# Activating A21 in place in PSUM, and sharing the four Winograd sums out anew between VectorE and GpSimd

## The chip, the cores and the metric

One core of a Trainium2 chip runs the kernel. The metric is device time in microseconds (us) of one execution. The engines are named as in the profile: PE is TensorE (its weight loads are listed apart, as PEld), DVE is VectorE, ACT is ScalarE, POOL is GpSimd, SP is SyncE, which only issues DMAs here. SBUF is the working memory. PSUM is the memory that PE writes its products to; it has eight banks of 512 fp32 columns over 128 partitions.

## The reference

```python
X = np.fft.fft(np.fft.fft(x, axis=1), axis=2).real     # x is 8 x 3008 x 256
h = X.reshape(24064, 256) @ w_in                        # w_in is 256 x 2048
g = h * (1.0 / (1.0 + np.exp(-1.702 * h)))              # quick gelu
return g @ w_out                                        # w_out is 2048 x 256
```

All of it is in fp32.

## The kernel before, in words

**Tiling.** The Fourier transform over the sequence is made by small matrix products (`mix1` and `stage2`), and the one over the 256 features is folded into `w_in` (tiles `wcs`). The rest, the two large products with the gelu between them, is cut into 384 steps. A step `t` is a batch (8), a block of rows (3), a half of it (2) and a place `p` in a group of 8 (line 508). A group shares one tile of output; its step number `p` handles hidden units 256p to 256p + 255 for 256 columns of rows (226 in one group of six). The first 8 steps use a plain form. This text is about steps 8 to 383, in the form below.

**A step.** The transform is symmetric, so each row comes with a mirrored row: the product with `wcs[0]` plus that with `wcs[1]` is the hidden value of one, their difference that of the other. A step has one PSUM bank, `b0` or `b1` by turns, called `x`. Five things happen to it, in this order:

- `middle(t)` (line 592, ACT): two instructions of 256 columns fill `x` with a correction term. I call this the **fill**.
- `begin(t)` (line 599 and the helper's line 184, PE): 8 matmuls add the product with `wcs[0]`.
- `doubled(t)` (line 604, ACT) copies twice that to a tile `g` in SBUF.
- `begin(t, 1)`: 8 more matmuls add the product with `wcs[1]`. `x` now holds the one half.
- `forward(t)` (line 607, ACT) writes the gelu of `x` to blocks A11 and A12 in SBUF. `backward(t)` (line 565, DVE) writes `g - x`, reversed in runs of 32, to blocks A21 and A22 in SBUF. `activate_back(t)` (line 614, ACT) takes the gelu of A21 and A22 in place, as one instruction of 512 columns.

**The sums.** The product with `w_out` is made by Winograd's form of Strassen's scheme, 2 x 2 blocks with seven products. It needs S1 = A21 + A22, S3 = A11 - A21, S2 = S1 - A11 and S4 = A12 - S2 (`sums`). Before, GpSimd makes S1 and S3 at each step (lines 622 and 623, 256 columns each), and VectorE makes S2 and S4 for two steps at once, one step after the odd one (lines 629 and 630, 512 columns each). One of the seven products is itself done by the same scheme over a pair of steps. Its four sums are made by `deeper` on VectorE (line 651, four instructions of 512 columns in each pair): s3, s1 and s2 two steps after the odd step of the pair, s4 one step later.

**Rings.** A11, A21, S3 and S2 lie in a ring of four steps ("left"), A12, S4, A22 and S1 in one of six ("right"). The products of step `t` are made at step `t + 3` (`LAG`).

**Order.** There is no planner: each engine has one queue, in the order of the calls in the loop at line 989. In a step `t` that order is:

- PE: `begin(t, 1)`; the first two of step t-3's large products; `begin(t+1)`; small products; the third large product. At p = 3 the order is another: small products come ahead of `begin(t+1)`.
- ACT: `forward(t)`; at p = 4 the three copies of `swap` (lines 794 to 796); `doubled(t+1)`; `activate_back(t)`; the fill for `t+2`; at p = 2 two copies (lines 754 and 756).
- DVE: `backward(t)`; at p = 3 the four instructions of `combine_small` (line 786); then at even `t` S2 and S4 of two steps and s4, at odd `t` s3, s1 and s2; at p = 2 lines 757 and 758, at p = 4 lines 768 and 804 (`combine_last`), at p = 5 and 6 a transpose (line 737).
- POOL: S1 and S3; in two groups of most batches also the folds of the next batch's input (`fold1`, lines 218 to 231).

A step at whose end `mix1` or `stage2` runs is *special*: that work uses the bank of step `t`, and the fill for `t+2` is issued at the start of the next step.

The fill for `t+2` writes the bank that step `t` used, so it waits until every reader of `x` of step `t` is done:

```python
x = xb[t] = bank("x", f"b{t % 2}")
```

Of the kernel before, what the change touches and what calls it, by code (L numbers as in the profile page):

```python
# [29 lines left out]
ALU = mybir.AluOpType  # L30
ACTF = mybir.ActivationFunctionType
# [19 lines left out]
def free(ap, offset, *dims):  # L51
    return bass.AP(ap.tensor, ap.offset + offset, [list(ap.ap[0])] + [list(d) for d in dims])
# [60 lines left out]
def kernel(ctx: ExitStack, tc, x, w_in, w_out, tab1, tab2, out):  # L113
    nc = tc.nc
# [12 lines left out]
    op = ctx.enter_context(tc.tile_pool(name="op", bufs=2, space=SB))  # L127
# [25 lines left out]
    big = cv.tile([128, 19 * 1024], F32, tag="big", name="big")  # L153
# [353 lines left out]
    NP = NF // 2  # L507
    steps = [(b, blk, hh, p) for b in range(B) for blk in range(NBLK) for hh in range(2) for p in range(NP)]
    vb, ht, xb, gt, pot = {}, {}, {}, {}, {}
    LEFT, MADE, RIGHT, SUM, RES, OUT = 0, 4096, 8192, 14336, 16384, 18432  # L510
    A11, A21, S3, S2 = range(4)
    A12, S4, A22, S1 = range(4)
# [3 lines left out]
    def width(t):  # L516

        return 226 if steps[t][1:3] == (0, 1) else 256
# [20 lines left out]
    def at_left(t, q):  # L539
        return LEFT + t % 4 * 1024 + q * 256  # L540

    def at_right(t, q):
        return RIGHT + (t // 2 % 3 * 2 + t % 2) * 1024 + q * 256

    def left(t, q, n):
        return big[:, at_left(t, q):at_left(t, q) + n]

    def right(t, q, n):
        return big[:, at_right(t, q):at_right(t, q) + n]
# [5 lines left out]
    def back(t):  # L555
        at = at_left(t, A21)
        return free(big[:], at, [at_right(t, A22) - at, 2], [1, width(t)])

    def reversed_sum(out, by, x, y, n, op):

        full, rest = divmod(n, RUN)
        for at, blocks, m in ((0, full, RUN), (full * RUN, 1, rest)):
            if m:
                ins = [free(z[:], at, [256, 2], [RUN, blocks], [1, m]) for z in (x, y)]
                nc.vector.tensor_tensor(free(out, at + m - 1, [by, 2], [RUN, blocks], [-1, m]), *ins, op=op)  # L565
# [19 lines left out]
    def middle(t):  # L585

        b, blk, hh, p = steps[t]
        n = width(t)
        x = xb[t] = bank("x", f"b{t % 2}")
        for i in range(2):  # L590
            f = 2 * p + i
            nc.scalar.activation(x[:, i * 256:i * 256 + n], nbt[b, blk][:, hh * 256:hh * 256 + n], ACTF.Copy,  # L592
                                 scale=af1[:, f:f + 1])

    def begin(t, cs=0):

        n = width(t)
        for i in range(2):
            halves(xb[t][:, i * 256:i * 256 + n], *operands(t, cs, i), start=False, stop=(cs == 1))
# [8 lines left out]

    def backward(t):
        at = at_left(t, A21)  # L610
        reversed_sum(big[:, at:at + 256], at_right(t, A22) - at, gt.pop(t), xb.pop(t), width(t), ALU.subtract)

    def activate_back(t):
        nc.scalar.activation(back(t), back(t), ACTF.Gelu_apprx_sigmoid)  # L614

    def sums(t, eng):

        if not NP <= t < len(steps):
            return
        n = width(t)  # L620
        if eng is nc.gpsimd:
            eng.tensor_tensor(right(t, S1, n), left(t, A21, n), right(t, A22, n), op=ALU.add)  # L622
            eng.tensor_tensor(left(t, S3, n), left(t, A11, n), left(t, A21, n), op=ALU.subtract)  # L623
            return
        if t % 2 == 0:
            return
        a11, s2 = (free(big[:], at_left(t - 1, q), [1024, 2], [1, n]) for q in (A11, S2))
        a12, s4, s1 = (free(big[:], at_right(t - 1, q), [1024, 2], [1, n]) for q in (A12, S4, S1))
        eng.tensor_tensor(s2, s1, a11, op=ALU.subtract)  # L629
        eng.tensor_tensor(s4, a12, s2, op=ALU.subtract)  # L630

    def deep(t):

        return NP <= t < last

    def raws(t, half):

        return free(big[:], at_right(t, 0) + half * (width(t) // 2), [256, 4], [1, width(t) // 2])

    def made_sum(q, w):  # L640
        return free(big[:], SUM + 512 * q, [128, 4], [1, w])

    def deeper(t, part):

        if t < 0 or not deep(t) or not steps[t][3] % 2:
            return
        s1, s2, s3, s4 = (made_sum(q, width(t) // 2) for q in range(4))
        a11, a12, a21, a22 = (raws(k, half) for half in range(2) for k in (t - 1, t))
        for out, i0, i1, how in (((s3, a11, a21, ALU.subtract), (s1, a21, a22, ALU.add), (s2, s1, a11, ALU.subtract)),
                                 ((s4, a12, s2, ALU.subtract),))[part]:  # L650
            nc.vector.tensor_tensor(out, i0, i1, op=how)  # L651

    SPOT = {2: 0, 6: 1, 5: 2, 7: 3, 3: 4, 4: 5}
# [282 lines left out]
    n = len(steps)  # L936
# [52 lines left out]
    for t in range(n + LAG):  # L989
        if t < NP:  # L990
            if t == NP - 3:
                spare[:] = [tag for tag in spare if tag[0] == "o"] + ["b2"]
            if t == NP - 1:
                middle(NP)
            hidden(t)
            if t == NP - 1:
                begin(NP)
                no_row(1024)
            if t == 0:
                squares(in2, nc.scalar)  # L1000
                nyquist(0, 0)
                low_up(in2)
                low_down(in2)
            if t in rows_at:
                first_row(rows_at[t])
            if t >= LAG and t != LAG + 1:
                product(t - LAG, 0, None)
            if t == LAG:
                product(1, 0, None)
            if t == 5:  # L1010
                bounds(("out", 2))
            if t == 6:
                low_down(("out", 3))
            if t:
                activate(t - 1)
            if t == 3:
                bounds(("in", 3))
            if t == 5:
                bounds(("out", 3), False)
            if t in early:  # L1020
                fold_w(early[t])
            rows(t)
            if t == NP - 1:
                doubled(NP)
                middle(NP + 1)
        else:
            after, special = (any(fn in (mix1, stage2) for fn, _ in extra.get(k, ())) for k in (t - 1, t))
            if t < n:
                begin(t, 1)
            if t == NP:  # L1030
                activate(t - 1)
            if after and t + 1 < n:
                middle(t + 1)
            if t < n:
                forward(t)
            while waiting:
                m, ps = waiting.pop()
                mixed(m, 1, ps)
            opening = (t - LAG) % NP == 0 and t >= NP + LAG
            one, other = (t - LAG, (1, 2, 4, 7)), (t - LAG - 1, (5, 6, 3))  # L1040
            if opening:
                small_products(*other)
            cut = 0 if opening and not after else 3 if after else 2
            product(t - LAG, 0, cut)
            if after:
                small_products(one[0], one[1][:1])
                small_products(other[0], () if opening else other[1][:1])
            if t + 1 < n:
                begin(t + 1)
            if not opening:  # L1050
                small_products(other[0], other[1][after:])
            product(t - LAG, cut, 6 if t - LAG == last else None)
            small_products(one[0], one[1][after:])
            swap(t - LAG - 2)
            if t < n:
                backward(t)
            if t + 1 < n:
                doubled(t + 1)
            if t < n:
                activate_back(t)  # L1060
                sums(t, nc.gpsimd)
            if t + 2 < n and not special:
                middle(t + 2)
            combine_small(t - LAG - 1)
            if t - LAG == last:
                product(last, 6, None)
            sums(t - 1, nc.vector)
            deeper(t - 2, 0)
            deeper(t - 3, 1)
        if t == NP:  # L1070
            psu.close()
            low = ctx.enter_context(tc.tile_pool(name="low", bufs=1, space=PS))
            pot["low"] = low.tile([128, 3 * 512], F32, tag="low", name="low")
        if t >= LAG:
            combine(t - LAG)
            combine_last(t - LAG - 2)
            turn_last(t - LAG - 3, 0)
            turn_last(t - LAG - 4, 1)
        if t >= NP:
            spare[:] = [f"b{t % 2}"] * special + ["b2"]  # L1080
        for fn, args in extra.get(t, ()):
            fn(*args)
# [28 lines left out]
```

## Time and profile before

| what | value |
|---|---|
| median of 3 runs | 1856.31 us (1854.34 to 1856.57) |
| the profiled execution: span from its first to its last instruction | 1853.1 us |
| granted TensorE clock, mean | 0.999 |
| busy in the span: PE, PEld, DVE, ACT, POOL | 99%, 76%, 82%, 62%, 53% |

The profile lists no time of its own for the profiled execution beside the span of 1853.1 us. That span is 3.2 us under the median of the runs, and 1.2 us under the fastest. Of the views, "groups" gives one kind of instruction a row (how many, mean duration, what ended the idle time before), "waits" sums up who waited for whom, "windows" gives busy time by stretch, and "timeline" the instructions in order with their start in us from the span's start. A row of the timeline may merge several instructions: x8 with 1.03 us are eight, from the start of the first to the end of the last. Consecutive instructions of one engine can overlap a little, so their starts are sometimes nearer than their durations.

### The profile page before, as it was taken

To read this page: it belongs to the slowest core of one execution; us is meant where nothing else is said; L and a number is where in the kernel's file an instruction comes from. 1 tells how busy PE (TensorE), PEld (TensorE's weight loads), DVE (VectorE), ACT (ScalarE), POOL (GpSimd) and SP (SyncE) were. 2 spreads that over 40 slices of the span, in tenths; PEclk is the share of its full clock that TensorE was granted. 3 is DMA by queue.
4 is the path that set the end of the run, shared out by engine and by line. 5 is a ranking of instruction groups with operands and counts; after the bars stand their busy time and mean duration, and the time that the engine had idled before them with its cause. 6 is when DMAs were issued, how large, how long until landed. Compare 5 with 4: busy or idle time off the path is not lost.

```text
span 1853.1 us, 56093 instructions
## 1 busy us (share of the span) xinstructions
PE 1836.6 (99%) x23722; PEld 1401.3 (76%) x23722; DVE 1520.9 (82%) x2222; ACT 1150.5 (62%) x2241; POOL 975.2 (53%) x1053
## 2 busy tenths in 40 slices
PE   8999999999999999999999999999999999999998
PEld 4677777777777777777777777777777777778776
DVE  6988778887798778987789878888888888878874
ACT  5666656665666666666566666666665666656663
POOL 4776446744368434773348643485445754444442
PEclk9999999999999999999999999999999999999999
DMA  8721340215012240223302132121411111100111
GB/s 280 181 61 34 85 67 19 72 52 99 19 46 48 73 81 13 52 50 90 57 13 67 43 86 52 19 75 35 103 31 23 37 46 36 31 19 13 23 19 24
DMA packets 149707, 105.31 MB, mean 57 GB/s; under 512 B 106057, under 2 KB 130665, under 8 KB 148896
## 3 DMA queue, kind: packets, MB, share of 16 engines
q1 hardware_dynamic: 146624, 99.68, 23.6%
q8 instruction: 187, 3.06, 0.7%
q10 hardware_dynamic: 2832, 2.05, 0.5%
q14 instruction: 64, 0.52, 0.1%
HBM read 64.41 MB, written 48.05 MB: 61 GB/s over the span
## 4 chain that ended last, share of the span: by engine, by line
PE 80%; DVE 9%; POOL 4%; ACT 2%; DMA 2%; issue 2%; SPq 0%; DVEq 0%; ACTq 0%; POOLq 0%
PE x L184 29%; PE o L184 22%; PE low L685 21%; PE o L685 3%; DVE big L651 3%; PE ps L255 2%; DVE big L786 2%; DVE big L565 1%; PE ps L365 1%; POOL xt L227 1%; DVE big L629 1%; POOL big L623 1%; DMA xt<-in_x_dram 1%; ACT big L607 1%; DMA Td<-big 1%
## 5 line engine op out<-in xcount | busy, mean ns | idle before, releaser
L622 POOL TENSOR_TENSOR big<-big 128x256 f32<-128x256 f32 (+1 forms) x376 | 353.0, 939 | 825.1 <-ACT big L614 691.4
L184 PE MATMUL x<-pq,wcs 128*64 128x256 f32 (+1 forms) x6016 | 768.8, 376 | 2.0 <-ACT g L604 1.4
L651 DVE TENSOR_TENSOR big<-big 128x512 f32<-128x512 f32 (+1 forms) x736 | 623.1, 861 | 23.4 <-PE low L685 4.7
L184 PE MATMUL o<-big,wo 128*64 128x256 f32 (+1 forms) x4800 | 620.8, 375 | 0.1
L184 PEld LDWEIGHTS x<-pq,wcs 128*64 128x64 f32 x6016 | 412.3, 137 | 186.0 <-issue 15.0
L184 PEld LDWEIGHTS o<-big,wo 128*64 128x64 f32 x4800 | 341.6, 137 | 148.0 <-DVE big L629 0.5
L604 ACT ACTIVATE g<-x 128x512 f32<-128x512 f32 (+1 forms) x376 | 221.6, 589 | 366.3 <-PE x L184 365.0
L565 DVE TENSOR_TENSOR big<-g,x 128x512 f32<-128x512 f32 (+2 forms) x440 | 254.1, 589 | 209.4 <-ACT big L607 209.0
L592 ACT ACTIVATE x<-nb,af 128x256 f32<-128x256 f32 (+1 forms) x752 | 352.9, 469 | 79.7 <-DVE pq L371 63.6
L685 PE MATMUL low<-big 128*64 128x128 f32 (+1 forms) x5888 | 382.8, 270 | 0.0
L685 PEld LDWEIGHTS low<-big 128*64 128x64 f32 x5888 | 337.5, 137 | 29.2
L623 POOL TENSOR_TENSOR big<-big 128x256 f32<-128x256 f32 (+1 forms) x376 | 352.6, 938 | 0.0
L607 ACT ACTIVATE big<-x 128x512 f32<-128x512 f32 (+1 forms) x376 | 219.2, 583 | 127.5 <-PE x L184 121.3
L614 ACT ACTIVATE big<-big 128x512 f32<-128x512 f32 (+1 forms) x376 | 231.9, 617 | 46.0 <-DVE big L565 44.0
L685 PE MATMUL low<-big,wo 128*64 128x128 f32 (+1 forms) x2944 | 220.4, 271 | 0.1
L685 PEld LDWEIGHTS low<-big,wo 128*64 128x64 f32 x2944 | 171.3, 137 | 4.2 <-DVE big L651 1.4
L630 DVE TENSOR_TENSOR big<-big 128x512 f32<-128x512 f32 (+1 forms) x188 | 160.8, 855 | 6.5
L629 DVE TENSOR_TENSOR big<-big 128x512 f32<-128x512 f32 (+1 forms) x188 | 137.3, 730 | 5.3 <-POOL big L622 5.3
L786 DVE TENSOR_TENSOR big<-big,low 128x512 f32<-128x512 f32 (+3 forms) x184 | 109.0, 609 | 3.5
L685 PEld LDWEIGHTS o<-big,wo 128*64 128x64 f32 x1472 | 92.2, 137 | 25.0
L685 PE MATMUL o<-big,wo 128*64 128x128 f32 (+1 forms) x1472 | 110.0, 270 | 0.0
L227 POOL TENSOR_TENSOR xt<-xt 111x510 f32<-111x510 f32 x56 | 86.0, 1535 | 4.4
(95 smaller groups left out, 966.2 us busy)
## 6 DMA issues: line engine op xcount, KB each, us to landing
out_dram<-os SPq DMA_DIRECT2D x284, 64.0 KB
t<-Td SPq DMA_DIRECT2D x22, 512.0 KB
Td<-xt SPq DMA_DIRECT2D x56, 192.0 KB
xt<-in_x_dram SPq DMA_DIRECT2D x14, 512.0 KB
xt<-Xr SPq DMA_DIRECT2D x14, 512.0 KB
nb<-Nd SPq DMA_DIRECT2D x23, 256.0 KB
out_dram<-os SPq DMA_DIRECT2D x96, 56.0 KB
Xr<-in_x_dram SPq DMA_DIRECT2D x7, 752.0 KB
```

The lines of the kernel that those rows point to most:

```text
L184: nc.tensor.matmul(out[c0:c0 + 64], lhsT=lhs[:, c0:c0 + 64], rhs=rhs, skip_group_check=True, **how)
L565: nc.vector.tensor_tensor(free(out, at + m - 1, [by, 2], [RUN, blocks], [-1, m]), *ins, op=op)
L592: nc.scalar.activation(x[:, i * 256:i * 256 + n], nbt[b, blk][:, hh * 256:hh * 256 + n], ACTF.Copy, scale=af1[:, f:f + 1])
L604: nc.scalar.activation(two(g[:], n), two(xb[t][:], n), ACTF.Copy, scale=2.0)
L607: nc.scalar.activation(front(t), two(xb[t][:], width(t)), ACTF.Gelu_apprx_sigmoid)
L614: nc.scalar.activation(back(t), back(t), ACTF.Gelu_apprx_sigmoid)
L622: eng.tensor_tensor(right(t, S1, n), left(t, A21, n), right(t, A22, n), op=ALU.add)
L623: eng.tensor_tensor(left(t, S3, n), left(t, A11, n), left(t, A21, n), op=ALU.subtract)
L629: eng.tensor_tensor(s2, s1, a11, op=ALU.subtract)
L630: eng.tensor_tensor(s4, a12, s2, op=ALU.subtract)
L651: nc.vector.tensor_tensor(out, i0, i1, op=how)
L685: nc.tensor.matmul(o, lhsT=lhs, rhs=rhs, start=first_in, stop=(p == NP - 2), skip_group_check=True)
```

## The change

The step's own PSUM bank takes the activated A21. `backward` still writes A21 and A22 to SBUF. `activate_back` becomes two instructions of 256 columns: the first reads A21 from SBUF and writes its gelu to the first 256 columns of `x`, the second does A22 in place in SBUF. In a special step `activate_back` stays as it was. S3 and S1, the two sums that read A21, move from GpSimd to VectorE, where A21 is read from PSUM. S2 and S4 move from VectorE to GpSimd. All four are made step by step, 256 columns each, in the step itself. On VectorE's queue s3 and s4 now stand ahead of S3 and S1, and s1 and s2 behind them and behind `combine_small`.

```diff
-        reversed_sum(..., gt.pop(t), xb.pop(t), width(t), ALU.subtract)
+        reversed_sum(..., gt.pop(t), xb[t], width(t), ALU.subtract)
-    def activate_back(t):
-        nc.scalar.activation(back(t), back(t), ACTF.Gelu_apprx_sigmoid)
+    def activate_back(t, there):
+        n = width(t)
+        x = xb.pop(t)
+        if not there:
+            nc.scalar.activation(back(t), back(t), ACTF.Gelu_apprx_sigmoid)
+            a21[t] = left(t, A21, n)
+            return
+        a21[t] = x[:, 0:n]
+        nc.scalar.activation(a21[t], left(t, A21, n), ACTF.Gelu_apprx_sigmoid)
+        nc.scalar.activation(right(t, A22, n), right(t, A22, n), ACTF.Gelu_apprx_sigmoid)
...
     def sums(t, eng):
...
-        if eng is nc.gpsimd:
-            eng.tensor_tensor(right(t, S1, n), left(t, A21, n), right(t, A22, n), op=ALU.add)
-            eng.tensor_tensor(left(t, S3, n), left(t, A11, n), left(t, A21, n), op=ALU.subtract)
-            return
-        if t % 2 == 0:
-            return
-        a11, s2 = (free(big[:], at_left(t - 1, q), [1024, 2], [1, n]) for q in (A11, S2))
-        a12, s4, s1 = (free(big[:], at_right(t - 1, q), [1024, 2], [1, n]) for q in (A12, S4, S1))
-        eng.tensor_tensor(s2, s1, a11, op=ALU.subtract)
-        eng.tensor_tensor(s4, a12, s2, op=ALU.subtract)
+        if eng is nc.vector:
+            a = a21.pop(t)
+            eng.tensor_tensor(left(t, S3, n), left(t, A11, n), a, op=ALU.subtract)
+            eng.tensor_tensor(right(t, S1, n), a, right(t, A22, n), op=ALU.add)
+            return
+        eng.tensor_tensor(left(t, S2, n), right(t, S1, n), left(t, A11, n), op=ALU.subtract)
+        eng.tensor_tensor(right(t, S4, n), right(t, A12, n), left(t, S2, n), op=ALU.subtract)
...
             if t < n:
-                activate_back(t)
+                activate_back(t, not special)
+            deeper(t - 2, 0, 0, 1)
+            deeper(t - 3, 1)
+            if t < n:
+                sums(t, nc.vector)
                 sums(t, nc.gpsimd)
             if t + 2 < n and not special:
                 middle(t + 2)
             combine_small(t - LAG - 1)
...
-            sums(t - 1, nc.vector)
-            deeper(t - 2, 0)
-            deeper(t - 3, 1)
+            deeper(t - 2, 0, 1)
```

(The two new arguments of `deeper` pick which of its instructions are issued.)

More of the change, by code (lines that the diff above doesn't have):

```diff
@@ L610, in backward @@
         at = at_left(t, A21)
-        reversed_sum(big[:, at:at + 256], at_right(t, A22) - at, gt.pop(t), xb.pop(t), width(t), ALU.subtract)
-    def activate_back(t):
-        nc.scalar.activation(back(t), back(t), ACTF.Gelu_apprx_sigmoid)
+        reversed_sum(big[:, at:at + 256], at_right(t, A22) - at, gt.pop(t), xb[t], width(t), ALU.subtract)
+    def activate_back(t, there):
[8 more added lines that the diff above has]
+        nc.scalar.activation(right(t, A22, n), right(t, A22, n), ACTF.Gelu_apprx_sigmoid)
+    a21 = {}
     def sums(t, eng):
-        if not NP <= t < len(steps):
+        if t >= len(steps):
             return
         n = width(t)
-        if eng is nc.gpsimd:
-            eng.tensor_tensor(right(t, S1, n), left(t, A21, n), right(t, A22, n), op=ALU.add)
-            eng.tensor_tensor(left(t, S3, n), left(t, A11, n), left(t, A21, n), op=ALU.subtract)
+        if eng is nc.vector:
+            a = a21.pop(t)
+            eng.tensor_tensor(left(t, S3, n), left(t, A11, n), a, op=ALU.subtract)
+            eng.tensor_tensor(right(t, S1, n), a, right(t, A22, n), op=ALU.add)
             return
-        if t % 2 == 0:
-            return
-        a11, s2 = (free(big[:], at_left(t - 1, q), [1024, 2], [1, n]) for q in (A11, S2))
-        a12, s4, s1 = (free(big[:], at_right(t - 1, q), [1024, 2], [1, n]) for q in (A12, S4, S1))
-        eng.tensor_tensor(s2, s1, a11, op=ALU.subtract)
-        eng.tensor_tensor(s4, a12, s2, op=ALU.subtract)
+        eng.tensor_tensor(left(t, S2, n), right(t, S1, n), left(t, A11, n), op=ALU.subtract)
+        eng.tensor_tensor(right(t, S4, n), right(t, A12, n), left(t, S2, n), op=ALU.subtract)
     def deep(t):
@@ L641, in made_sum, with deeper @@
         return free(big[:], SUM + 512 * q, [128, 4], [1, w])
-    def deeper(t, part):
+    def deeper(t, part, lo=0, hi=None):
         if t < 0 or not deep(t) or not steps[t][3] % 2:
@@ L649, in deeper @@
         for out, i0, i1, how in (((s3, a11, a21, ALU.subtract), (s1, a21, a22, ALU.add), (s2, s1, a11, ALU.subtract)),
-                                 ((s4, a12, s2, ALU.subtract),))[part]:
+                                 ((s4, a12, s2, ALU.subtract),))[part][lo:hi]:
             nc.vector.tensor_tensor(out, i0, i1, op=how)
```

## The prediction

> **What bounds the kernel now.** I read the page's busy shares first, then the stretches, then the waits.
>
> ```profile
> PE 1836.6 (99%) x23722; PEld 1401.3 (76%) x23722; DVE 1520.9 (82%) x2222; ACT 1150.5 (62%) x2241; POOL 975.2 (53%) x1053
> ```
>
> PE has no room. The view of stretches shows where its little idle time lies:
>
> ```profile
> 0.00:50.00 50.00, 44.19 (x408) 25.62 (x410) 34.45 (x49) 30.65 (x47) 21.44 (x22) 1.00 0.90 290
> ...
> 300.00:500.00 200.00, 199.25 (x2660) 154.22 (x2658) 168.21 (x246) 125.01 (x247) 111.76 (x122) 1.00 0.28 60
> ```
>
> In the steps PE lacks 0.75 us of 200. The kernel is as long as PE's matmuls, and the change touches none of them. So the question is only whether PE starts to wait. The waits tell for whom it already does, a little:
>
> ```profile
> POOL big L622 <- ACT big L614: 691.4, 291, 5.3
> ...
> PEld x L184 <- ACT x L592: 8.6, 33, 0.7
> ```
>
> GpSimd's long wait costs nothing: its sums are read three steps later. The second row is the place to watch: PE's weight load waits for ACT's fill of bank `x`. The timeline shows one such place, at p = 5 of a group (columns: start, us, engine, line):
>
> ```profile
> 861.17 0.68 DVE L565 TENSOR_TENSOR big<-g,x 128x512 f32<-128x512 f32 x1
> ...
> 861.89 0.63 ACT L614 ACTIVATE big<-big 128x512 f32<-128x512 f32 x1 [0.98 <-DVE big L565]
> 862.43 0.97 ACT L592 ACTIVATE x<-nb,af 128x256 f32<-128x256 f32 x2
> ...
> 863.45 0.63 PEld L184 LDWEIGHTS x<-pq,wcs 128*64 128x64 f32 x8 [0.23 <-ACT x L592]
> 863.51 1.03 PE L184 MATMUL x<-pq,wcs 128*64 128x256 f32 x8
> ```
>
> `backward` is late on DVE, so `activate_back` and the fill are late, and the matmuls start just in time. Over all steps I took, from the trace, the distance from the end of a fill's first half to the first matmul on it. It is never under 0.54 us, and at 0.54 PE had waited; so what is over 0.54 is **spare**. The median spare by p = 0 to 7 is 0.62, 0.87, 2.05, 0.72, 0.63, 0.08, 1.31, 1.15 us.
>
> **What the change does to this chain.** Before, the fill follows `activate_back` directly on ACT. After, it waits for S1 on DVE, because S3 and S1 read the bank. Behind the waiting fill on ACT's queue stands `forward(t+1)`, and on that waits the next `backward`.
>
> Durations. Half an activation: line 614 takes 625 ns for 512 columns and 577 for 452, so 0.8 ns a column and 0.42 us for 256; the second starts 0.35 after the first, since ACT's instructions overlap by 0.1. The PSUM write is not in the trace for this function. It is bounded by 0.365 (line 754, 256 columns from PSUM) and 0.625 (the whole instruction); I take 0.42, near line 592's 0.473, which writes 256 columns to PSUM. S3 and S1: 0.42 each, as lines 757 and 758 (256 columns, one input in PSUM; 377 to 422 ns). Bounds: 0.38, and 0.95, what GpSimd took for the same sums. They start 0.35 apart.
>
> So on an idle DVE the fill starts 0.35 + 0.42 + 0.03 (second half), then S1's 0.42 and 0.03, that is 1.25 us after `activate_back` begins, in place of 0.5: **0.75 later**. Against the spare that leaves p = 1, 2, 6, 7 whole, p = 3 short by 0.03, p = 4 by 0.12, p = 5 by 0.67. That is 0.8 us a group, if nothing else moves.
>
> But DVE's queue moves too. S2 and S4 leave it (before 0.73 + 0.78 for two steps), four sums of 0.42 come for two steps, so DVE's total hardly changes (+0.2 us a pair). The order does change: s1 and s2 now stand behind S1, and `combine_small` behind S1, too. I work one boundary out, in the trace's own times: p = 3 begins at 848.35, p = 4 at 852.68, p = 5 at 857.45.
>
> ```profile
> 851.66 0.60 ACT L604 ACTIVATE g<-x 128x512 f32<-128x512 f32 x1 [1.58 <-PE x L184]
> 852.16 0.62 ACT L614 ACTIVATE big<-big 128x512 f32<-128x512 f32 x1
> 852.67 0.98 ACT L592 ACTIVATE x<-nb,af 128x256 f32<-128x256 f32 x2
> ...
> 854.44 0.62 ACT L794 COPY big<-big 64x512 f32<-64x512 f32 x1
> ...
> 856.38 0.60 ACT L604 ACTIVATE g<-x 128x512 f32<-128x512 f32 x1
> 857.00 0.63 ACT L614 ACTIVATE big<-big 128x512 f32<-128x512 f32 x1
> ```
>
> ```profile
> 850.12 0.69 DVE L565 TENSOR_TENSOR big<-g,x 128x512 f32<-128x512 f32 x1 [0.39 <-ACT big L607]
> 850.74 2.46 DVE L786 TENSOR_TENSOR big<-big,low 128x512 f32<-128x512 f32 x4
> 853.12 2.88 DVE L651 TENSOR_TENSOR big<-big 128x512 f32<-128x512 f32 x3
> 855.91 0.68 DVE L565 TENSOR_TENSOR big<-g,x 128x512 f32<-128x512 f32 x1
> ```
>
> These are ACT's and DVE's queues. See that `combine_small` (L786) starts at 850.74 now. After:
>
> 1. The first half of `activate_back` starts at 852.16 as before (`doubled` waits for PE). S3 at 852.61, S1 at 852.96 to 853.38, the fill's first half 853.41 to 853.88. PE wants it by 853.87: just met.
> 2. `combine_small` starts at 853.31, 2.57 later than now, and ends at 855.77. s1 at 855.69, s2 at 856.41 (0.72 apart, as lines 629 and 630), `backward` at 857.03 to 857.71, s4 to 858.34.
> 3. `swap` reads what `combine_small` makes. It starts at 855.80, and `doubled` 1.94 later as now (854.44 to 856.38): 857.74. `activate_back` at 858.24, S3 at 858.69, S1 859.04 to 859.46, the fill's first half to 859.96, the matmuls 0.54 later: 860.50. PE would have had them at 852.68 + 6.50 = 859.18. **PE waits 1.32 us.**
> 4. p = 5 has this 1.32 as its own cover. Lines 768 and 804 run from 859.39 to 861.58 (spaced as now), `backward` to 862.26, S1 to 863.59, the fill's first half to 864.09; the matmuls could start at 864.63, and PE comes at 863.51 + 1.32 = 864.83. No more is lost, and p = 6 and 7 have over a microsecond each.
>
> What of the rest: S2 and S4 on GpSimd (0.73 to 1.18 each) start at S1's end, and the first reader is 1.5 steps or more away; cost 0, and if that cover went, as in a fold step, still behind the 3 steps of the ring. No DMA moves past another.
>
> **The sum.** 46 group boundaries have `combine_small`. 14 of them have a special step at p = 3 or 4, where the extra PE work gives time back; I take 0.8 there, between 0.3 and 1.3. 32 x 1.32 = 42, 14 x 0.8 = 11. In the 8 groups of 226 columns PE's step is shorter; in one of them (762 to 782 us) the distances at p = 1, 3, 5 are 0.92, 1.03, 0.82, so the spare 0.28 to 0.49, and 0.67 more is asked: 8 x 3 x 0.3 = 7. Where GpSimd folds, s3 ahead of S3 may have to sit out line 227 (1.535 us) on an odd step: some 56 steps, at 0.1: 6. Together 66: a span of 1853.1 + 66 = 1919, and 3.2 more for the median: **1922 us**.
>
> The Trainium skill's "SBUF — State Buffer" (its practical consequences on the shared ports) says that a VectorE instruction with two SBUF inputs and a GpSimd instruction that reads SBUF exclude each other for the whole instruction. By it s1 and s2, which now run just when S1 has released S2 and S4, would take up to 0.69 + 0.73 each; if that held at p = 3, `backward` would end at 859.1 and the wait be 2.2 in place of 1.32. Here line 651 took 0.68 alone and 1.22 beside GpSimd, and at p = 3 `combine_small` gives S2 and S4 time to end first; so I keep 1.32.
>
> **Rivals.**
> - *The wait is in every pair.* If S3 and S1 take 0.9 each (GpSimd's row), the fill of an ordinary odd step is ready at 3.82 + 1.7 + 0.5 + 0.54 = 6.54 us after its step began, and PE wants it at 6.06. Some 138 odd steps x 0.48 = 66 more: **1988**. It decides once the two take over 1.2 together. For it: line 629 went up to 2.9 us in single cases. Against: line 757 never passed 0.422. Chance 0.18.
> - *Faster.* S3 and S1 with a PSUM input may no longer hinder GpSimd, line 651's mean falls from 0.86 towards 0.68, and DVE is early enough at p = 4 and 5 to feed `backward`. It needs `combine_small` to run 1.3 us earlier than in my step 2. Then what PE waits now goes: 4.7 us by the stretches from 100 to 1800, at most some 17 by PEld's waits for ACT and DVE in the steps. Price -5 to -17, **1845**. Chance 0.12. (The skill's "Perfetto Trace Analysis", "Identifying the Most-Contended Engine", holds that matmul busy time is a poor measure of room on PE; by it the 17 would be nearer than the 4.7.)
> - *The order holds.* The fill is late by tenths only, since DVE works faster than I space it: 0 to 0.4 a group, **1856 to 1875**. Chance 0.10, of which 0.04 within 0.2% (about what a measurement of this kernel tells from no change).
>
> **How the numbers follow.** My forecast has 0.60: 1885 (0.8 a group less the special ones) to 1955 (2.2 a boundary). Range 1868 to 1980: it leaves out the faster case, the unchanged one and the top of the first rival, 0.2 in all. Faster 0.12; same 0.04; slower 0.60 + 0.18 + 0.06 = 0.84.
>
> **What would show it.** Right: PE (or PEld) on line 184, tile `x`, waits some 40 to 70 us for line 592, mostly once a group, at p = 4 to 5; the fill waits for DVE's S1; `swap` starts some 2 to 3 us later in its group. Wrong: waits spread over all odd steps (first rival); PE at 99% as before (third); or PE waiting for another line.

## The result, and the profile after

The changed kernel takes 1925.15 us (median of 4 runs, 1923.75 to 1925.49), the kernel before 1855.7 beside it: a ratio of 1.0375, with a 95% interval of 1.036 to 1.0389. It is 69.5 us slower. The profiled execution has a span of 1923.2 us, 70.1 more than before.

The busy shares of the changed kernel, from its page:

```profile
PE 1863.8 (97%) x23722; PEld 1392.7 (72%) x23722; DVE 1463.9 (76%) x2598; ACT 1193.3 (62%) x2566; POOL 925.0 (48%) x1053
```

Two things are to be seen. VectorE and GpSimd are less busy than before, by 57 and 50 us: the change did relieve them, and the kernel is slower all the same. And PE's busy time *grew* by 27 us, with the same 23722 matmuls. The bars of matmuls that follow one another overlap in the trace: each is 0.38 us long, and two start every 0.22 us. Where PE waits, the end of the last bar stands alone and counts as busy, and the first bar after the wait is longer (0.43 us). In step p = 4 of the group shown below, 0.87 us longer than before, 0.65 show as idle and 0.22 as busy. So 27 of the 70 us that PE lost are counted as busy; only the other 43 show as idle. "97%" hides most of a loss of 3.7%. Weight loads kept their sum (1401 and 1393 us) and fell from 76% to 72%, which tells it better. (The Trainium skill, "Perfetto Trace Analysis", section "Identifying the Most-Contended Engine", says that matmul busy time is a poor measure of how close a kernel is to the chip's limit, and names two in its place, of which the share of weight loads is one; this case agrees with that.)

The view of stretches, with the columns sum, PE, PEld, DVE, ACT, POOL, clock, DMA share, GB/s:

```profile
0.00:50.00 50.00, 44.30 (x408) 25.40 (x410) 34.29 (x49) 30.50 (x47) 21.40 (x22) 1.00 0.90 287
300.00:500.00 200.00, 194.23 (x2540) 145.82 (x2536) 155.45 (x278) 125.47 (x273) 101.32 (x118) 1.00 0.26 58
```

The opening is as before; in the steps PE makes 2540 matmuls in 200 us where it made 2660. The clock is 1.00 as before. The waits name what PE waits for:

```profile
POOL big L637 <- DVE big L635: 914.8, 348, 6.9
...
ACT x L592 <- DVE big L635: 165.6, 323, 1.4
...
PEld x L184 <- ACT x L592: 70.1, 128, 1.9
...
ACT big L802 <- DVE big L794: 34.2, 39, 1.0
...
PEld x L184 <- ACT g L604: 30.9, 45, 1.2
...
PE x L184 <- ACT g L604: 21.4, 37, 1.0
...
PE x L184 <- ACT x L592: 15.1, 46, 1.5
...
PE ps L255 <- DVE big L565: 5.7, 7, 0.8
```

The fill (L592) now waits for S1 (L635), 323 times. PE waits for the fill, as forecast. It also waits for `doubled` (L604), 45 times by its weight loads, about once a group: that wait was not in the forecast. `swap` (L802) waits for `combine_small` (L794). The last row is `mix1`, at p = 4 of seven groups with a special step: it takes the step's bank and waits for `backward` to have read it.

To see where the time went I took the length of every step, from the first matmul of `begin(t, 1)` to that of the next step, and subtracted the same step's length before. Summed by the place p of the step in its group:

| p | 0 | 1 | 2 | 3 | 4 | 5 | 6 | 7 | all |
|---|---|---|---|---|---|---|---|---|---|
| us longer in all | -0.1 | 2.6 | 9.4 | 0.5 | 32.1 | 20.3 | 3.6 | 1.2 | 69.7 |
| median of a step | 0.00 | 0.00 | 0.26 | 0.00 | 0.87 | 0.55 | 0.00 | 0.00 | |

One boundary in the timeline of the changed kernel, the same group that the prediction worked out (p = 3 begins at 876.81, p = 4 at 881.14, p = 5 at 886.78):

```profile
881.03 0.42 DVE L634 TENSOR_TENSOR big<-big,x 128x256 f32<-128x256 f32 x1 [0.95 <-ACT x L622]
...
881.37 0.42 DVE L635 TENSOR_TENSOR big<-x,big 128x256 f32<-128x256 f32 x1
881.70 2.46 DVE L794 TENSOR_TENSOR big<-big,low 128x512 f32<-128x512 f32 x4
...
881.82 0.99 ACT L592 ACTIVATE x<-nb,af 128x256 f32<-128x256 f32 x2 [0.49 <-DVE big L635]
...
884.19 0.62 ACT L802 COPY big<-big 64x512 f32<-64x512 f32 x1 [0.86 <-DVE big L794]
...
885.40 0.68 DVE L565 TENSOR_TENSOR big<-g,x 128x512 f32<-128x512 f32 x1
...
886.13 0.60 ACT L604 ACTIVATE g<-x 128x512 f32<-128x512 f32 x1
886.75 0.39 ACT L622 ACTIVATE x<-big 128x256 f32<-128x256 f32 x1
...
886.78 1.08 PE L184 MATMUL x<-pq,wcs 128*64 128x256 f32 x8 [0.65 <-ACT g L604]
...
887.17 0.42 DVE L634 TENSOR_TENSOR big<-big,x 128x256 f32<-128x256 f32 x1 [0.49 <-ACT x L622]
...
887.51 0.42 DVE L635 TENSOR_TENSOR big<-x,big 128x256 f32<-128x256 f32 x1
...
887.97 0.99 ACT L592 ACTIVATE x<-nb,af 128x256 f32<-128x256 f32 x2 [0.49 <-DVE big L635]
...
889.01 1.08 PE L184 MATMUL x<-pq,wcs 128*64 128x256 f32 x8 [0.28 <-ACT x L592]
```

`combine_small` stands behind S3 and S1; `swap` waits for it; `doubled` stands behind `swap`; and `begin(t+1, 1)` may not write the bank before `doubled` has read it, so PE waits at 886.78. The first half of `activate_back` (L622) stands behind the same `doubled`; S3 waits for it, the fill waits for S1, and PE waits once more, for the fill, at 889.01.

### The profile page after: what moved, and what is told of

Read it like the earlier page. It is cut to its first block, busy times and chain, and to the rows that moved or that the text cites. A ratio compares the mean times of both kernels' runs of the same rounds, so it can differ in the third digit from the quotient of the medians.

```text
span 1923.2 us, 56983 instructions
## 1 busy us (share of the span) xinstructions
PE 1863.8 (97%) x23722; PEld 1392.7 (72%) x23722; DVE 1463.9 (76%) x2598; ACT 1193.3 (62%) x2566; POOL 925.0 (48%) x1053
## 4 chain that ended last, share of the span: by engine, by line
PE 67%; ACT 15%; DVE 11%; DMA 3%; issue 2%; POOL 0%; SPq 0%; ACTq 0%; DVEq 0%; POOLq 0%
PE x L184 26%; PE low L693 19%; PE o L184 16%; DVE big L794 5%; ACT x L592 4%; PE o L693 3%; ACT g L604 3%; DVE big L635 2%; DVE big L659 2%; ACT big L623 2%; ACT x L622 2%; PE ps L255 1%; DMA xt<-in_x_dram 1%; PE ps L365 1%; ACT big L802 1%
## 5 line engine op out<-in xcount | busy, mean ns | idle before, releaser
L637 POOL TENSOR_TENSOR big<-big 128x256 f32<-128x256 f32 (+1 forms) x376 | 332.4, 884 | 916.3 <-DVE big L635 914.8
L659 DVE TENSOR_TENSOR big<-big 128x512 f32<-128x512 f32 (+1 forms) x736 | 591.9, 804 | 16.7 <-PE x L184 0.9
L184 PEld LDWEIGHTS x<-pq,wcs 128*64 128x64 f32 x6016 | 402.1, 137 | 261.3 <-ACT x L592 70.1
L592 ACT ACTIVATE x<-nb,af 128x256 f32<-128x256 f32 (+1 forms) x752 | 356.4, 474 | 241.1 <-DVE big L635 165.6
L604 ACT ACTIVATE g<-x 128x512 f32<-128x512 f32 (+1 forms) x376 | 221.9, 590 | 337.5 <-PE x L184 334.9
L565 DVE TENSOR_TENSOR big<-g,x 128x512 f32<-128x512 f32 (+2 forms) x440 | 254.6, 590 | 149.9 <-ACT big L607 149.8
L638 POOL TENSOR_TENSOR big<-big 128x256 f32<-128x256 f32 (+1 forms) x376 | 342.3, 910 | 29.5
L634 DVE TENSOR_TENSOR big<-big,x 128x256 f32<-128x256 f32 (+1 forms) x325 | 135.1, 416 | 144.3 <-ACT x L622 141.7
L607 ACT ACTIVATE big<-x 128x512 f32<-128x512 f32 (+1 forms) x376 | 216.8, 577 | 23.6 <-PE x L184 20.3
L635 DVE TENSOR_TENSOR big<-x,big 128x256 f32<-128x256 f32 (+1 forms) x325 | 134.7, 414 | 0.1
L623 ACT ACTIVATE big<-big 128x256 f32<-128x256 f32 (+1 forms) x325 | 130.8, 402 | 0.0
L622 ACT ACTIVATE x<-big 128x256 f32<-128x256 f32 (+1 forms) x325 | 123.5, 380 | 8.8 <-DVE big L565 7.6
L794 DVE TENSOR_TENSOR big<-big,low 128x512 f32<-128x512 f32 (+3 forms) x184 | 108.7, 608 | 3.4
```

The source lines that it names most:

```text
L184: nc.tensor.matmul(out[c0:c0 + 64], lhsT=lhs[:, c0:c0 + 64], rhs=rhs, skip_group_check=True, **how)
L604: nc.scalar.activation(two(g[:], n), two(xb[t][:], n), ACTF.Copy, scale=2.0)
L607: nc.scalar.activation(front(t), two(xb[t][:], width(t)), ACTF.Gelu_apprx_sigmoid)
L623: nc.scalar.activation(right(t, A22, n), right(t, A22, n), ACTF.Gelu_apprx_sigmoid)
L635: eng.tensor_tensor(right(t, S1, n), a, right(t, A22, n), op=ALU.add)
L637: eng.tensor_tensor(left(t, S2, n), right(t, S1, n), left(t, A11, n), op=ALU.subtract)
```

## The experiments

The theory: at the group boundary two chains run, each over its own queue, and PE waits for the later one. Chain A is `combine_small` on VectorE, then `swap` and `doubled` on ACT; from `doubled` it reaches PE twice, directly and through `activate_back`, S3, S1 and the fill. Chain B is `combine_small`, s1, s2, `backward`, s4, S3, S1 on VectorE, then the fill. The rivals are that holding the bank costs at every step, and that the new instructions cost by themselves. Times are medians, each against the kernel before on the same chip (1854.6 to 1855.4 us).

**1. `swap` behind the fill** (`combine_last` and the transposes one step later, since they read what `swap` makes).

```diff
-            swap(t - LAG - 2)
...
             if t + 2 < n and not special:
                 middle(t + 2)
+            swap(t - LAG - 2)
```

> The changed kernel with the three copies of swap moved on ACT's queue from ahead of doubled to behind the fill for t+2, and combine_last and the two transposes after it one step later. Theory (two queues at the group boundary, whichever is later): at p = 4 doubled no longer stands behind swap, so PE's wait for doubled (30 us in all) goes. What is left is DVE's own chain at that place: combine_small, s1, s2, backward, s4, S3, S1, fill; it makes the fill about 0.87 us late a group instead of some 1.4 in all. Some 0.5 x 46 = 23 us come back: 1902, between 1895 and 1910. Rival (what costs is only that the fill waits for S1 in the step's own bank): swap is not on the path, 1920 to 1925. Rival (it is only swap): all comes back, 1856 to 1862.

Measured: 1996.6 us, ratio 1.076 (1.0742 to 1.0778). All three missed. PE's loss at p = 4 did fall, from 32 to 4 us, but p = 5, 6 and 7 lost 41, 34 and 48. The timeline of this kernel shows one reason:

```profile
956.87 0.99 ACT L592 ACTIVATE x<-nb,af 128x256 f32<-128x256 f32 x2 [0.55 <-DVE big L635]
957.88 0.62 ACT L802 COPY big<-big 64x512 f32<-64x512 f32 x1
958.53 0.62 ACT L803 COPY big<-big 64x512 f32<-64x512 f32 x1
959.18 0.61 ACT L804 COPY big<-big 64x512 f32<-64x512 f32 x1
959.82 0.60 ACT L607 ACTIVATE big<-x 128x512 f32<-128x512 f32 x1
```

Behind the fill `swap` is ahead of the next `forward` (L607), which the late fill had already pushed back. It is 1.9 us in front of another chain: the next `backward` (at 960.45) waits 3.53 us for that `forward`. The move does not take `swap` off the path; run 7 does that. It also puts `combine_last` ahead of `backward` one step later, where `activate_back` then waits 1.62 us for `backward` (at 966.88). How the losses at p = 6 and 7 divide between the two is not shown.

**2. and 3. s1 and s2 one step later; both moves together.**

```diff
-            deeper(t - 3, 1)
...
-            deeper(t - 2, 0, 1)
+            deeper(t - 3, 0, 1)
+            deeper(t - 3, 1)
```

> The changed kernel with s1 and s2 of deeper moved from the end of the odd step to the end of the next step, just ahead of s4, which moves with them. Theory (two queues at the boundary): backward at p = 4 comes 1.4 us earlier, but PE waits there for doubled behind swap first, and the first half of activate_back stands behind the same doubled; so next to nothing comes back: 1918 to 1925. Rival (DVE's backlog ahead of backward alone sets the loss): 1860 to 1880.

> Both moves of the two kernels before together. Theory: with swap out of doubled's way and s1 and s2 out of backward's way, the fill for p = 6 is ready at about 5.9 us after p = 4 began and PE wants it at 6.5: no wait at the boundary is left. What stays is the narrow groups and single steps: 1856 to 1864, though the two moves alone give 23 and about 0. Rival (the fill's wait for S1 costs in every step): not under 1885.

Measured: 2117.7 us (1.1415; 1.1397 to 1.1433) and 1983.8 us (1.069; 1.0674 to 1.0706). Both theories missed, by far. The third number does lie in the open range of its rival ("not under 1885"), but its loss does not look like one of every step: it is 48 us at p = 3, 29 each at p = 1 and p = 6, and about nothing at p = 4, 5 and 7. The sums now end in an even step and hold up `backward` of the odd one, and s4 has become late for PE itself. The timeline of the third kernel, at p = 3 (942.55):

```profile
942.23 2.96 DVE L659 TENSOR_TENSOR big<-big 128x512 f32<-128x512 f32 x3
...
945.96 0.68 DVE L565 TENSOR_TENSOR big<-g,x 128x512 f32<-128x512 f32 x1
```

```profile
945.25 0.66 PE L693 MATMUL low<-big,wo 128*64 128x128 f32 x8 [0.48 <-DVE big L659]
```

PE's small products wait for s4 there, and the loss at p = 3, next to nothing in the changed kernel, is 48 us. These three runs do not decide on the theory: each edit put the work ahead of something else that was late. In runs 1 and 3, where `swap` is out of `doubled`'s way, the loss at p = 4 does go (from 32 to 4 and to -2 us), and in run 2 it stays (25). Runs 7 to 9 take work out instead.

**4. No bank held.** A21 is activated in SBUF, as before; everything else as changed.

```diff
-                activate_back(t, not special)
+                activate_back(t, False)
```

> The changed kernel with A21 activated in SBUF as before (one ACT instruction of 512 columns, no bank held), all the rest as changed: S3 and S1 on VectorE from SBUF, S2 and S4 on GpSimd, the new order on DVE's queue. Theory: combine_small still stands behind S3 and S1, so swap and doubled at p = 4 are as late as in the changed kernel, and PE waits about 0.9 to 1.0 us a group for doubled; the fill no longer waits for S1 and stays within that cover. Some 46 us over the kernel before: 1900, between 1890 and 1910. Rival (holding the bank is what costs): 1854 to 1865.

Measured: 1901.4 us, ratio 1.0249 (1.0233 to 1.0264): as expected. Two thirds of the loss, 46 us, is there without the bank, nearly all at p = 4 (43 us), and PE waits for `doubled`, as its waits say:

```profile
PEld x L184 <- ACT g L604: 40.1, 46, 1.4
...
PEld x L184 <- ACT x L592: 4.8, 9, 1.9
```

**5. No bank held, and `combine_small` back behind `backward`.**

```diff
             if t < n:
                 backward(t)
+            combine_small(t - LAG - 1)
...
-            combine_small(t - LAG - 1)
```

(and the line of run 4)

> A21 activated in SBUF as before (no bank held), and combine_small put back directly behind backward on DVE's queue; S3 and S1 stay on VectorE, S2 and S4 on GpSimd, step by step. Theory (without the bank held, the whole loss is combine_small standing behind S3 and S1): combine_small starts at p = 3 where it did before, swap and doubled are on time, and no wait is left: 1855, between 1850 and 1860. Rival (the new placing of the four sums costs DVE time of its own): 1870 or more.

Measured: 1852.95 us (10 runs) against 1855.43, ratio 0.9984 (0.9975 to 0.9994). The whole loss is gone, so the new placing of the four sums costs nothing by itself. The interval lies below 1: this version is faster than the changed kernel and, by 0.16%, than the one before. That is under the 0.2% that the prediction called no change. VectorE's and ACT's queues at its boundary (p = 3 from 885.52, p = 4 from 889.85):

```profile
887.28 0.69 DVE L565 TENSOR_TENSOR big<-g,x 128x512 f32<-128x512 f32 x1 [0.39 <-ACT big L607]
887.91 2.46 DVE L794 TENSOR_TENSOR big<-big,low 128x512 f32<-128x512 f32 x4
...
893.31 0.67 DVE L565 TENSOR_TENSOR big<-g,x 128x512 f32<-128x512 f32 x1
```

```profile
891.62 0.62 ACT L802 COPY big<-big 64x512 f32<-64x512 f32 x1
...
893.56 0.60 ACT L604 ACTIVATE g<-x 128x512 f32<-128x512 f32 x1
```

`combine_small` follows `backward` again, and `doubled` starts at 3.71 us after p = 4 began, as in the kernel before (3.70), not at 4.99. By step length the gain is at p = 4 (2.6 us), in six groups with a special step, 0.2 to 0.6 us each. There `mix1` waited for `backward` by 0.5 us (before: five times and 2.5 us in the waits, `PE ps L255 <- DVE big L565`), and here that row is gone from PE's waits; its weight loads still wait, for `deeper` (2.5 us in all) and `combine_small` (2.3).

**6. The bank held, and `combine_small` back behind `backward`** (the diff of run 5 alone).

> The changed kernel, bank held, with combine_small put back directly behind backward. Theory (the fill's wait for S1 and combine_small compete for the same stretch of DVE): the loss only moves. At p = 3 S1 ends 2.5 us later, so the fill for p = 5 is some 1.4 us late and PE waits for it in step p = 4; swap and doubled are on time. 46 x 1.4 is about what is saved: 1918, between 1900 and 1932. Rival (the order's loss and the bank's loss simply add, 46 and 24): 1879.

Measured: 1947.5 us, ratio 1.0497 (1.048 to 1.0515). Not additive, as the theory has it, but 15 us over its range. p = 4 lost 57.8 us, 1.37 in the median, where 1.4 was expected; p = 5 lost another 0.53, which I had left out. ACT's queue there, p = 4 from 931.32:

```profile
933.32 0.99 ACT L592 ACTIVATE x<-nb,af 128x256 f32<-128x256 f32 x2 [1.82 <-DVE big L635]
934.25 0.58 ACT L607 ACTIVATE big<-x 128x512 f32<-128x512 f32 x1
934.85 0.62 ACT L802 COPY big<-big 64x512 f32<-64x512 f32 x1
...
936.79 0.60 ACT L604 ACTIVATE g<-x 128x512 f32<-128x512 f32 x1
```

The late fill (1.82 us of waiting for S1) holds up `forward` behind it, that holds up `swap`, and `swap` holds up `doubled`: it starts 5.47 us after p = 4 began (3.70 in the kernel before), where the expectation had it on time. The four kernels make a table, in us over the kernel before:

| | `combine_small` behind `backward` | behind S3 and S1 |
|---|---|---|
| no bank held | -2.5 | 46.3 |
| bank held | 92.1 | 69.5 (the change) |

With the bank held, the change's late `combine_small` is the better place of these two. With no bank held, it is all of the loss. So the 69.5 us can't be divided into a share of the order and a share of the bank: holding the bank costs 23 us in the one order and 95 in the other.

**7. to 9. Work taken out.** Without `swap`; without `swap` and without s1 and s2 at p = 3; without s1 and s2 at p = 3 alone.

```diff
-            swap(t - LAG - 2)
...
-            deeper(t - 2, 0, 1)
+            if t % NP != 3 or t < 24:
+                deeper(t - 2, 0, 1)
```

> The changed kernel without the three copies of swap: this leaves out part of the computation, the exchange of the halves of the inner scheme's results. Nothing else moves on any queue. Theory (two chains at p = 4, the later one counts): doubled is on time, and DVE's own chain is left, combine_small, s1, s2, backward, s4, S3, S1, fill, 0.87 us late where both together were some 1.4: 1900, between 1890 and 1908. Rival (swap alone): 1870 or less. Rival (DVE's chain alone): 1920 to 1926.

> As the kernel before, and also without s1 and s2 at p = 3 in each group (two of the 16 sums that the inner scheme makes in a group are left out, and the products read the ones of the pair before). Theory: backward at p = 4 comes 1.4 us earlier, so the second chain is gone as well; what stays is p = 2 (9 us) and single places: 1868, between 1858 and 1878. Rival (the fill's wait for S1 costs at every step): not under 1885.

> The changed kernel without s1 and s2 at p = 3 in each group, swap kept (two of the 16 sums that the inner scheme makes in a group are left out). Theory (two chains at p = 4, the later one counts): doubled still stands behind swap, and the first half of activate_back behind doubled, so nothing comes back though VectorE has 1.4 us less to do ahead of backward: 1922, between 1915 and 1927. Rival (the two chains add): 1925 less 31, the step from no swap to no swap and no s1 and s2: 1894.

Measured: 1901.3, 1870.0 and 1922.6 us; ratios 1.0247 (1.0231 to 1.0262), 1.0077 (1.0062 to 1.0092) and 1.0366 (1.035 to 1.0381). All three as the theory had them. PEld's waits, of run 7:

```profile
PEld x L184 <- ACT x L592: 75.8, 127, 1.9
```

of run 8:

```profile
PEld x L184 <- ACT x L592: 43.5, 96, 2.3
```

with its fill's wait for S1,

```profile
ACT x L592 <- DVE big L635: 166.1, 323, 1.4
```

and of run 9:

```profile
PEld x L184 <- ACT x L592: 71.3, 131, 1.9
...
PEld x L184 <- ACT g L604: 33.1, 51, 1.2
```

Without `swap` the wait for `doubled` is gone and the fill's is left; without s1 and s2 alone both stay. In a plain group whose p = 2 loses nothing, the loss by step length is 1.42 us in the changed kernel, about 0.84 without `swap`, 1.42 without s1 and s2, and 0.05 without both. That is the later of two chains, A with 1.42 and B with 0.84, and not their sum. Run 8 also rules out a price at every step: the fill waits for S1 there 323 times, as in the changed kernel, and 15 us of 70 are left.

**10. The kernel before, with `activate_back` in two halves**, nothing else.

```diff
-        nc.scalar.activation(back(t), back(t), ACTF.Gelu_apprx_sigmoid)
+        for half in (left(t, A21, width(t)), right(t, A22, width(t))):
+            nc.scalar.activation(half, half, ACTF.Gelu_apprx_sigmoid)
```

> The kernel before with activate_back as two instructions of 256 columns, both in SBUF; nothing else is changed. Theory (an ACT instruction costs only what it pushes the fill past its spare): the halves take 0.38 and 0.41 with starts 0.31 apart, so the fill starts 0.10 later; the spare is least at p = 5, 0.08, so at most some hundredths a group: 1856, between 1853 and 1860. Rival (ACT's extra 0.17 us a step is on the path of every step): 376 x 0.17 = 64 more, 1919.

Measured: 1860.9 us, ratio 1.0034 (1.0022 to 1.0047), a little over my range and far from the rival. 4.8 us are lost in step p = 6, 0.13 to 0.19 in each of 28 groups, at the matmuls on the fill of p = 5: the place with a spare of 0.08 us. The other places together lost 0.6. In the worked group that fill starts 0.18 us later than before: 0.09 come from the two instructions, as I had it, and 0.09 from `backward`, which itself starts later there. The second part I had left out. The instruction's row, by form:

```profile
L615 ACT ACTIVATE big<-big 128x256 f32<-128x256 f32 x624 | 223.8, 408 | 36.5 <-DVE big L565 32.7
```

Each half takes 0.41 us, where I had put 0.38 and 0.41.

## Why the prediction was right

**The sum.** 66 us were forecast, 69.5 measured, 1922 against 1925.15. The mechanism, the fill late at the boundary and PE waiting for it, held; that the total came this close is luck in part, since its smaller terms were wrong in both directions.

**Steps 1 to 3, the boundary.** In the worked group everything fell within 0.1 us of its place. Counted from the start of p = 4: `combine_small` begins at 0.56 us (forecast 0.63), `backward` at 4.26 (4.35), `swap` at 3.05 (3.12), `doubled` at 4.99 (5.06), S1 ends at 6.79 (6.78), the fill's first half at 7.30 (7.28), its matmuls start at 7.87 (7.82). PE would have started them at 6.50. The wait is 1.37 us, forecast 1.32. The durations held: S3 and S1 0.42 us each, the half activation into PSUM 0.38 where I took 0.42. One sign that I had named, `swap` 2 to 3 us later, contradicts step 3: that has it 1.36 later, and it came 1.29 later (it is `combine_small` that moved by 2.5).

**Where PE waits.** Here the working failed in part. It let PE wait once, for the fill, and missed that `begin(t+1, 1)` waits for `doubled`. In the group above PE stops first there, for 0.87 us, and then 0.50 us for the fill. The sum is the same, because the fill's end comes from ACT's and VectorE's queues and does not move when PE stops earlier. But the forecast's own sign of an error ("PE waiting for another line") came up: at p = 4 PE's matmuls waited for `doubled` at 31 of the 32 boundaries without a special step and at 6 of the other 14, and the theory had to be widened. Without that wait run 4 could not be explained: no bank is held there, and 46 us are lost. At seven boundaries with a special step PE waited for yet another, `mix1` for `backward` (5.7 us).

**The terms of the sum.** By step length, in us over the kernel before:

| place | forecast | measured |
|---|---|---|
| p = 4 and 5, the 32 boundaries without a special step | 42 | 44.2 |
| p = 4 and 5, the 14 with one | 11 | 7.5 |
| p = 2, all groups | (a part of the 13) | 9.4 |
| all other steps | 13: narrow groups (226 columns) 7, folds 6 | 8.6 |

The boundary terms held: 53 forecast, 51.7 measured. The loss at p = 2 is the term that I had at nothing in the wide groups. 5.4 of the 9.4 us lie in 15 of the 32 groups without a special step at p = 3 or 4, some 0.36 each: the groups whose p = 0 is special (`stage2`). In one of them the distance at p = 1 was 0.95 us in the kernel before (step from 839.09), a spare of 0.41, and the change asks for 0.75. I had used the median spare of p = 1, 0.87, which lies in the other kind of step. Without the bank p = 2 loses 0.0 (run 4), with it 9.5 behind the other order, too (run 6): here the held bank is the cause. The distance of 0.92 that I read in a narrow group belongs here too: its p = 0 is special as well.

The term for the narrow groups, 7 us, came out as 5.3 at their p = 2 and p = 6. In the seven wide groups with folds at p = 1 and 2 these two places lost 3.7 us together; whether the folds cost them is not shown. Another 1.8 us are one step, p = 3 of the last group, where a large product waits for `combine_small`.

**VectorE's load.** "DVE's total hardly changes" was wrong: its busy time fell by 57 us. Summed over the instructions, durations fell by 27 (`deeper` 42 less, its mean from 861 to 804 ns; VectorE's two of the four sums 17 more); the other 30 are more overlap between consecutive instructions, of which there are 376 more. Two of its rows after:

```profile
L659 DVE TENSOR_TENSOR big<-big 128x512 f32<-128x512 f32 (+1 forms) x736 | 591.9, 804 | 16.7 <-PE x L184 0.9
...
L634 DVE TENSOR_TENSOR big<-big,x 128x256 f32<-128x256 f32 (+1 forms) x325 | 135.1, 416 | 144.3 <-ACT x L622 141.7
```

The faster rival had the shorter `deeper` right, but not its reason: in run 5, where S3 and S1 read SBUF alone, the mean is 800 ns. It needed `combine_small` to come early as well, and run 5, though without the input in PSUM, shows what that is worth: 2.5 us, less than the 5 to 17 that I named.

**The rival of a wait in every pair** fell: S3 and S1 with an input in PSUM took 0.38 to 0.42 us (longest 0.425 of 650), not 0.9, and the median loss at p = 0, 1, 6 and 7 is 0.00. (In its price, 3.82 + 1.7 + 0.5 + 0.54 is 6.56, not 6.54, so 69 us and not 66.)

**GpSimd and the DMAs** cost nothing, as forecast: the only rows of PE's waits that name them, one of 2.0 and one of 1.2 us, stand with the same numbers in the kernel before.

## What to carry to other kernels

A relieved engine pays nothing where its load was hidden; what a change does to the *order* of the queues decides, and the place to look is the step with the most work, not the mean one. Find for each buffer of the bound engine the spare (how long before its use it is ready), separately for each kind of step, add what the change delays, and follow the late instruction to all that stands behind it on its queue. When a buffer is held longer, its next writer waits at the head of an in-order queue, and everything behind waits with it.

## What the runs showed of the hardware

- S3 and S1 with one input in PSUM did not mind GpSimd: 71 of the 650 ran beside one of its instructions, and none of these took over 0.423 us (0.425 for the others). The same two sums with both inputs in SBUF (run 5) took 0.38 to 0.43 us alone; beside GpSimd, 108 of them, 0.70 to 1.05 in the mean by sum and width, and up to 1.54. The Trainium skill, "SBUF — State Buffer", in its practical consequences on the shared ports, says that an instruction with at most one SBUF input does not contend; this agrees.
- The contention moved rather than went: `combine_last`'s 768-column sum (line 812, before 804) went from 0.97 to 1.35 us, since S2 and S4 now run beside it. In run 1, which moves it one step on, it took 0.96 us wherever GpSimd had ended before (at 965.29, for one).
- ACT's gelu of 256 columns from SBUF took 0.383 us into PSUM and 0.406 into SBUF in the same kernel. The skill's "ScalarE: Activation LUTs" (in its step-by-step part) calls PSUM the lower-latency destination; here that is 0.02 us.
- PE's busy time can rise by waiting: by 27 us here with the same matmuls, while their weight loads kept theirs (1401 and 1393 us).
